# Both batches' tokens side by side, scores from loaded keys and means of V in 32-column tiles

## The chip, the cores and the metric

One Trainium2 chip, one of its cores. The metric is the device time of one execution in microseconds (us), taken as the median of the runs shown.

## The reference

Three blocks in a row, for 2 batches of 768 tokens; all matrices are float32 or float64 cut to what the kernel loads.

- **Attention**, 8 heads of 64. Each token attends to the tokens less than 16 away and to 24 summaries of the sequence, one per block of 32 tokens: the key of a summary is the elementwise maximum of the block's keys, its value the mean of the block's values, and log(32) is added to its score. Scores are scaled by 1/8, one softmax goes over both kinds.
- **Layer 1** (tokens x 512): `h = relu(x @ w_in)`, 1024 wide, cut into u and v; v is normalised over its 512 columns, mixed over tokens by a 768x768 matrix plus a bias per token, and multiplied with u; then `@ w_out`.
- **Layer 2**: `h = relu(x @ w_in2)`, 1024 wide; a convolution of three taps over tokens, per column; `h * sigmoid(conv)`; then `@ w_out2`.

`x @ w_out @ w_in2` has no nonlinearity between, so the kernel multiplies the two weights once (`merge`).

## The kernel before

Dense products are float32 with nearly full precision: each operand is a rounded high part and a low part (the rest), and `mm3` (lines 305 to 311) issues three products for one: high by high, high by low, low by high. `convert` (287 to 303) turns a float64 weight into both parts: one load, a ScalarE or GpSimd multiplication (293, 294), three VectorE steps (296, 298, 300), a cast (284) and a subtraction (278).

Attention goes over 8 pairs of heads (4 per batch), with 2 groups of 6 blocks of 64 queries per pair, so 16 groups.

- `load_kq`, `load_values` (355 to 376): loads of k, q and V's windows, and of v by columns for pairs whose means are not made by TensorE.
- `keys` (378 to 406): `win` copies and scales the windows of 94 keys of a group next to each other (387 on ScalarE, 389 on GpSimd), `top` takes the maxima of 32 keys (397), `put` copies the 24 maxima behind each window (403). So a block has one key matrix of 118 columns.
- `means` (408 to 438): for pairs 0 and 2 (`MEANS_PE`) 12 products with 24 columns of weights (417), all 128 rows of the array; for the others a VectorE sum (424) and a transposition (427). 429, 434 and 436 copy the result.
- `group` (446 to 523): `qk` puts log(32) and the masks into the score bank by small bfloat16 products (460, 466) and adds the score products (473; a float32 product leaves two records in the trace), maxima (477), exponentials with sums (481), reciprocals (487), normalisation (490), transposes (494) and their copies (516), output products (500), high and low parts of the output (521, 522).

Then `f1u`, `f1v` (layer 1's first product), `spatial` (the mixing), `merge`, `i2` (layer 2's first product, its convolution in 684, sigmoid 687, gate 690, high and low part) and `o2` (last product, 709 and 710 write it out). A dense piece is 512 or 256 columns wide: a batch's 768 tokens are cut by `TS` into 512 and 256.

The order on the engines is written out by hand: every `add` call is one job with the engines that could do it; two signs of the string `ORDER` name one job by its number (64 times the first sign's place in `SIGNS` plus the second's), so that counting `add` calls decodes it; a digit of `PICK` names the engine where there is a choice. Each engine, and SP's queue of loads, takes its jobs in that order. Where the plan sees TensorE without work for 0.5 us, it puts in padding: products of constants (720) that nobody reads, the same that warm TensorE up at the start.

Of the kernel before, what the change touches and what calls it, by code (L numbers as in the profile page):

```python
# [29 lines left out]
GB = 6  # L30
GA = GB // 2
NG = NB // GB
MK = 5 * WK + 2 * QB + GA * NS
NZ = NS - 2
# [4 lines left out]
TS = [slice(0, 512), slice(512, S)]  # L39
SLOT = 1536  # L40
MEANS_PE = (0,2)
# [11 lines left out]
    "ACAAABAFAEAgAGADAiAjASATAkAUAhAVAWAXAHAqArALBaAMBbAYBZAIAZA3A4AaBcAbBYAsAcAtAuAvANBiBjAJAlBECTAdA5A6AOBvAwBFCUBwCSA7BkBl"  # L53
    "AKAmBmB8DJAnCRAxAyBxDHCVBGCbA8AzA9A+AoA0BnA-B9DKAPBHCoByBzCcBdDLApBKBLA1A2DIB0BABoCpBpC1BBEgCdEhBCBDCeBqBrB+DRBMCfCgB1B2"
    "BeAQBfBhCqB3B-BIDeBRBgBsEfBSDSDTBJB4ChCrCiCsEeCtCDCEDfDgCWBtBuCXCYCKARB5CjCkC2E0BTBUBVBNCaCuCvBOCFCGCHB6B7BPDUCZClCmCwCx"
    "EnETCMDVDhFODiDWFMDXDYCnCyCAEoEpEUFBC5DMCIBQDwDxDZDrCzC0DNDOCJDyDaDjDkEqErFPFVC6DQE1DPCBDbDlE2DmC3DsC7C8DtDnC9C+AeFNEsDc"
    "DdCCDoFWFXE3E4FiDpEtDqEuC-DuDvDzEiEvD0EjFYEkAfBWCLBXE5D1CNCOF7CPCQD6D7D2D3EwD4E6DADBFjD8ElC4F6ExF8F9EVFCFvGmGDFkGQDCDDEX"
    "DEEZEmEYEaFZEbE7D5D9D+D-EAE8EBDFDGEcE9EEEFEGEHECFFGnFGFzFaFbEIEOEPEQEyGEEzFHGkGdJ5FwEWFIEdFlFcFdERF0FJF1F2F3FeE+E-EDEJEK"
    "ELEMGlESHRFKFLHSFmFQFAFRFDFEGFGRF4FnF5FoENHHHTHIGfFpGGGeFqHJGgGHFSGhGiFrFTFfFgFhGSG6GtGjFUGuGTGUF+FsFtHUHVFuHKHLGIGJHlHb"
    "HcHWGVG7GKGLHdF-HeHmHnGvGwGMGWHoGAGBGNGxGyHXG8HMHNGCFxFyGoHfGXGYIiGZHpHqG9GOGPHrIyIDHvGzHwGaH5HgHsGbGcG0G1H6GpJ9GqIzHxHy"  # L60
    "IjG+G-G2HAGsGrG3HzHOHPG4HtH0H7HBItG5HCH8IEHhHiIFHDHQISJ+H9IIHjHuHYKEJ-HkHZKLIaKAHEINIJITHFHGI0IGIKI1IUILIdIOIeIkIVIPIfIg"
    "IHIMI9I+IbH+KBKCHaH1H2H-IAKDIcI3IBICIXH3KGKFIlI-IWIhKSKHKIIQJlJbIRImJ6KJH4KNKKIYKMI2IZKOI4InKPIoKQJmJvJnJHJIJJJKI5JLIuIv"
    "JAJMKRKjJwJcJoJdJRJSIwJxJTJeIqIrIpJNJOKUKTJBK3K4JUKtJCJPKVKWIsJDJEKXIxLpLrKYJyK5KkKlJpJqI6I7I8LqLsJVJFJWJfJgLtKuK6JGKmLu"
    "JzKnKZKaKvKwKoK7LLLvJXJYJrLwLyJZJhJaLxLzL0JiL1JQJ8L3JjJ0L2KpKxKbKcKdLMLBK8LfLCJsKqL5LgKeLVMrKyLhLWKfMhLiLNL4JkJtL6L7LjLk"
# [12 lines left out]
)
PICK = (
    "001110111100001000001011101001100101011101111100000100000001111101100010001100010000100120001100100110001100110110000010"
    "10000001111011110022000011000000010010010000100100010000110010000100100110100001000000"  # L80
# [121 lines left out]
def block_kernel(ctx, tc, q_in, k_in, vwin, v_in, w_in, w_spT, b_sp, w_outT, w_in2, conv, w_out2, out):  # L202
# [23 lines left out]
    sx, sw, sv0, sar, ssp, stmp = [slots(f"x{b}", NP) for b in range(B)], slots("w", 6), slots("v", 6), slots("a", 14), slots("sp", 1), slots("tmp", 1, 2560)  # L226
    X = [bufs(s) for s in sx]
# [97 lines left out]
    kws, kss, sts = [carve(k, NB * NK) for k in (4, 5)], [carve(k, 32) for k in (4, 5)], [carve(k, 24) for k in (4, 5, 4, 5)]  # L325
    qts, vts = [carve(k, S) for k in (6, 7)], [carve(k, S) for k in (6, 7)]
    kts, ptss, vss = [carve(k, S + 2 * HK) for k in (8, 9)], [carve(10, 128 * GB) for _ in range(2)], [carve(11, 128) for _ in range(2)]
    es = [carve(k, GB * NK + 16) for k in (8, 9, 11, 13)]
    vzs, mask_b, runs_t = [carve(12, NS) for _ in range(2)], carve(12, MK // 2 + 8), carve(12, 2 * NS - 2)
    assert max(used) <= SLOT  # L330
    mask_m = mask_b.ap[:, :MK // 2].bitcast(BF16)
    masks, one, three, logs = mask_m[:, :5 * WK], mask_m[:, 5 * WK:5 * WK + QB], mask_m[:, 5 * WK + QB:5 * WK + 2 * QB], mask_m[:, 5 * WK + 2 * QB:]
# [18 lines left out]

    def vw_tok(j, g, sub):
        return vws[j].tok(g * GB * 128, (g + 1) * GB * 128, sub)

    def load_kq(n):
# [5 lines left out]
        for i, (k0, k1) in enumerate(cuts):  # L361
            dma((k1 - k0) / 2, lambda k0=k0, k1=k1: SP.dma_start(kts[j].ap[:, k0:k1], k_in[b, p][:, k0:k1]), r - 12 + 0.5 * i, writes=[kts[j].tok(k0, k1)])
# [15 lines left out]
    def keys(n):  # L378

        j, r = n % 2, STEP * NG * n  # L380
        for g in range(NG):
            def win(eng, g=g):
                t = kts[j].ap
# [7 lines left out]
            add({"POOL": (0.66, lambda win=win: win(POOL)), "ACT": (0.7, lambda win=win: win(ACT)), "DVE": (0.44, lambda win=win: win(DVE))}, r - 4 + STEP * g,  # L391
                [kts[j].tok(g * GB * QB, (g + 1) * GB * QB + 2 * HK)], [kw_tok(j, g)], lock=True)

        parts = 2 if n < NP and KPART else 1
        for i in range(parts):
            def top(i=i, w=S // parts):
                DVE.tensor_reduce(out=kss[j].ap[:, w // 32 * i:w // 32 * (i + 1)], in_=kts[j].ap[:, HK + w * i:HK + w * (i + 1)].rearrange("p (n k) -> p n k", k=32), op=ALU.max, axis=AX.X)

            w = S // parts
            add({"DVE": (0.14 + w / 960, top)}, r - 4, [kts[j].tok(HK + w * i, HK + w * (i + 1))], [kss[j].tok(w // 32 * i, w // 32 * (i + 1))])  # L400

        def put(eng):
            eng.tensor_scalar(out=kw3(j)[:, :, :NS], in0=kss[j].ap[:, :NS].unsqueeze(1).to_broadcast([128, NB, NS]), scalar1=SCALE, scalar2=0.0,
# [470 lines left out]
```

## Time and profile before

| | us |
|---|---|
| median of 3 runs | 335.71 (335.19 to 336.82) |
| profiled execution | 334.98 |
| its span, first to last instruction | 333.2 |
| TensorE busy in the span | 328.4 |
| VectorE, ScalarE, GpSimd busy | 239.8, 184.6, 82.0 |

The granted clock of TensorE is full over the whole span. Times in the profile are counted from the span's start. Busy TensorE is counted with modelled ends of its products, so that the distance from start to start, not the duration, tells what one costs.

### The profile page before, as it was taken

Reading aid. Unit: us, or ns where it says so; the run is one execution under the profiler, and the core shown is the slowest. Engines: PE = TensorE matmul, PEld = TensorE weight load, DVE = VectorE, ACT = ScalarE, POOL = GpSimd, SP = SyncE. Lnnn points to the kernel's source line nnn. Section 1 sums busy time; section 2 is a strip of 40 time slices with the busy share of each in tenths; the row PEclk is TensorE's granted clock in tenths of the full one; section 3 lists DMA queues with packets and bytes.
Section 4 is the critical chain, followed back from the end, with each engine's and each line's share of the span. In section 5 each row is a group of like instructions: output and inputs, shape, how many; then the busy total and the mean of one; then the engine's idle time right before and its main releaser. Section 6 shows DMA issues by size and latency. Waiting matters only on the chain.

```text
span 333.2 us, 6369 instructions
## 1 busy us (share of the span) xinstructions
PE 328.4 (99%) x2488; PEld 274.6 (82%) x2488; DVE 239.8 (72%) x432; ACT 184.6 (55%) x459; POOL 82.0 (25%) x94
## 2 busy tenths in 40 slices
PE   8999999999999999999999999999999999999996
PEld 3678888888888888888888888888888888888885
DVE  7889899876887599698869687898958542385400
ACT  4999996957245754243325246856664454464221
POOL 4795773334110133200010100351021222011000
PEclk9999999999999999999999999999999999999999
DMA  6999954931253541312302330300000010010023
GB/s 211 317 294 357 249 168 142 275 110 27 63 173 109 211 157 63 128 50 79 126 0 75 116 126 14 114 0 4 0 0 2 0 63 33 0 63 2 0 94 126
DMA packets 13325, 34.49 MB, mean 104 GB/s; under 512 B 1648, under 2 KB 3952, under 8 KB 13296
## 3 DMA queue, kind: packets, MB, share of 16 engines
q1 hardware_dynamic: 13296, 34.10, 32.3%
q8 instruction: 19, 0.31, 0.4%
q14 instruction: 10, 0.08, 0.1%
HBM read 30.95 MB, written 3.15 MB: 102 GB/s over the span
## 4 chain that ended last, share of the span: by engine, by line
PE 97%; DMA 2%; SPq 0%; DVE 0%; issue 0%; ACT 0%
PE late L310 12%; PE late L309 12%; PE late L311 12%; PE mm L309 10%; PE mm L310 9%; PE mm L311 9%; PE xp L500 4%; PE pt L494 4%; PE xp L309 3%; PE xp L310 3%; PE xp L311 3%; PE s L473 3%; PE pt L310 3%; PE pt L309 3%; PE pt L311 3%; PE mm L417 2%
## 5 line engine op out<-in xcount | busy, mean ns | idle before, releaser
L684 DVE SCALAR_TENSOR_TENSOR x<-x,conv_t 128x767 f32<-128x767 f32 x32 | 37.8, 1187 | 14.7 <-ACT x L681 14.3
L481 ACT ACTIVATE a<-s,a 128x118 f32<-128x118 f32 x96 | 33.0, 367 | 1.2 <-DVE a L477 0.9
L298 DVE SCALAR_TENSOR_TENSOR a<-a,a 128x512 uint32<-128x512 uint32 (+1 forms) x32 | 21.6, 674 | 5.5 <-ACT a L293 4.2
L293 ACT ACTIVATE a<-a 128x512 f32<-128x512 f32 (+1 forms) x26 | 17.0, 655 | 10.7 <-DVE w L278 2.8
L278 POOL TENSOR_TENSOR w<-a,w 128x256 fp32r<-128x256 f32 (+1 forms) x11 | 10.4, 949 | 44.2 <-ACT w L284 44.0
L481 ACT ACTIVATION_READ_ACCUMULATOR a<-s,a 128x1 f32 x96 | 20.6, 214 | 0.0
L300 DVE SCALAR_TENSOR_TENSOR a<-a,a 128x512 uint32<-128x512 uint32 (+1 forms) x32 | 19.9, 623 | 0.8
L687 ACT ACTIVATE x<-x 128x768 f32<-128x768 f32 x16 | 13.4, 846 | 12.4 <-DVE x L684 12.3
L490 POOL TENSOR_TENSOR a<-a,a 128x708 f32<-128x708 f32 x13 | 17.9, 1378 | 2.9 <-ACT a L481 1.5
L284 ACT CAST w<-a 128x512 fp32r<-128x512 f32 (+1 forms) x14 | 8.0, 576 | 18.3 <-DVE a L300 18.3
L309 PE MATMUL mm<-w,x 128*128 128x512 f32 x40 | 16.7, 418 | 0.0
L494 PE MATMUL pt<-ident,a 128*118 128x128 f32 x96 | 16.5, 280 | 0.2 <-DVE a L516 0.2
L690 DVE TENSOR_TENSOR x<-x 128x768 f32<-128x768 f32 x11 | 10.5, 956 | 8.4 <-ACT x L687 8.3
L681 ACT ACTIVATE x<-x,conv_t 128x768 f32<-128x768 f32 x16 | 14.7, 939 | 2.6 <-POOL w L278 1.3
L311 PE MATMUL mm<-w,x 128*128 128x512 f32 x40 | 15.7, 392 | 0.0
L310 PE MATMUL mm<-w,x 128*128 128x512 f32 x40 | 15.7, 392 | 0.0
L690 POOL TENSOR_TENSOR x<-x 128x768 f32<-128x768 f32 x5 | 10.1, 2016 | 21.9 <-ACT x L687 21.9
L477 DVE TENSOR_REDUCE a<-s 128x6 f32<-128x708 f32 x16 | 14.1, 883 | 1.8 <-PE s L473 1.5
L500 PEld LDWEIGHTS xp<-a,a 118*64 118x64 f32 x384 | 12.5, 137 | 3.4 <-issue 2.5
L500 PE MATMUL xp<-a,a 118*64 118x64 f32 x384 | 14.7, 226 | 0.0
L309 PE MATMUL mm<-x,w 128*128 128x256 f32 (+1 forms) x40 | 14.7, 367 | 0.0
L494 PEld LDWEIGHTS pt<-ident,a 128*118 128x118 f32 x96 | 10.8, 136 | 4.1 <-issue 0.8
(323 smaller groups left out, 1079.8 us busy)
## 6 DMA issues: line engine op xcount, KB each, us to landing
a<-w_in SPq DMA_DIRECT2D x12, 512.0 KB, 3.8
a<-w_out SPq DMA_DIRECT2D x8, 512.0 KB, 4.0
out<-tmp SPq DMA_DIRECT2D x11, 256.0 KB, 2.0
a<-vwin SPq DMA_DIRECT2D x8, 288.0 KB, 5.9
a<-v_in SPq DMA_DIRECT2D x6, 384.0 KB, 6.7
a<-vwin SPq DMA_DIRECT2D x4, 576.0 KB, 6.7
tmp<-w_spT SPq DMA_DIRECT2D x6, 384.0 KB, 3.4
a<-w_in SPq DMA_DIRECT2D x8, 256.0 KB, 5.1
```

The lines of the kernel that those rows point to most:

```text
L293: mul = {"ACT": (0.2 + n / 1080, lambda: ACT.mul(fu.f(), half(1).bitcast(F32), 2.0 ** -112)), "POOL": (0.12 + n / 1050, lambda: POOL.tenso ...
L298: add({"DVE": (0.16 + n / 960, lambda: DVE.scalar_tensor_tensor(out=last.u(), in0=fu.u(), scalar=0x80000000, in1=last.u(), op0=ALU.bitwise ...
L300: add({"DVE": (0.16 + n / 960, lambda: DVE.scalar_tensor_tensor(out=fu.u(), in0=fu.u(), scalar=3, in1=last.u(), op0=ALU.logical_shift_left ...
L309: PE.matmul(ps, lhsT=lh, rhs=rh, start=first and i == 0, stop=False)
L310: PE.matmul(ps, lhsT=lh, rhs=rl, start=False, stop=False)
L311: PE.matmul(ps, lhsT=ll, rhs=rh, start=False, stop=last and i == n - 1)
L481: ACT.activation(out=e[:, u, :NK], in_=sv[:, u // GA, u % GA], func=AF.Exp, bias=st[:, 0, u:u + 1], scale=1.0, accum_out=sm[:, u, :1])
L490: eng.tensor_tensor(out=e, in0=e, in1=st[:, 1].unsqueeze(2).to_broadcast([128, GB, NK]), op=ALU.mult)
L494: PE.transpose(pt3[:NK, a], e[:, GA * h + a, :NK], ident)
L500: PE.matmul(xp[h * D:(h + 1) * D, k * QB:(k + 1) * QB], lhsT=vw3(j)[:NK, g * GB + k, h * D:(h + 1) * D], rhs=pts[:NK, at:at + QB], start=T ...
L684: DVE.scalar_tensor_tensor(out=ct.f()[:, to], in0=hh.f()[:, of], scalar=conv_t[:, 3 * f + k:3 * f + k + 1], in1=ct.f()[:, to], op0=ALU.mul ...
L690: eng.tensor_tensor(out=ct.f(), in0=hh.f(), in1=ct.f(), op=ALU.mult)
```

## The change

- **Tokens side by side.** The attention output is kept as four buffers of high parts and four of low parts, each with both batches' 768 tokens in a row (1536 columns), in place of a buffer per batch and pair with high and low. The mixing writes its result into the same buffers. Layer 2's first product then runs over all 1536 tokens in three pieces of 512 (`k` = 0, 1, 2); the 256 columns of piece 1 that belong to batch 1 are kept in `hb` and joined later (`join`).
- **Keys without copies.** For the pairs in `DIRECT` (batch 0) `win` and `put` go. A block's scores come from the loaded keys (94 columns) and from the maxima (24 columns) by two products in place of one of 118. Nothing has scaled these keys, so the constants are put in unscaled (`many`, masks of -8e9), the maximum is scaled by one more VectorE step and the exponential scales its input. Four key buffers serve in place of two (two of them lie where the windows of batch 0 were).
- **Means in tiles.** Pair 1 joins pairs 0 and 2 in `MEANS_PE`, so that its v isn't loaded. Pairs 1 and 2 (not 0) use weights of 32 columns in four column tiles of the array, by block number modulo 4; ScalarE copies the 128x128 result and one more product with the matrix `comb` adds the four parts.
- **Buffers and order.** Weights and gate results of the later layers lie elsewhere, `ORDER` and `PICK` are new throughout.

```diff
+DIRECT = (0,1,2,3)
+MEANS_F = (0,)
-TS = [slice(0, 512), slice(512, S)]
+TS = [[slice(0, 512), slice(512, S)], [slice(0, 256), slice(256, S)]]
-MEANS_PE = (0,2)
+MEANS_PE = (0,1,2)
...
-    kws, kss, sts = [carve(k, NB * NK) for k in (4, 5)], [carve(k, 32) for k in (4, 5)], [carve(k, 24) for k in (4, 5, 4, 5)]
+    kws, kss, sts = [carve(k, NB * NK) for k in (4, 5)], [carve(k, 32) for k in (4, 5, 4, 5)], [carve(k, 24) for k in (4, 5, 4, 5)]
...
+    def kt(n):
+        return kts[n % (4 if n in DIRECT else 2)]
...
-        for g in range(NG):
+        for g in range(0 if n in DIRECT else NG):
             def win(eng, g=g):
...
+        if n not in DIRECT:
+            add({"POOL": (0.44, lambda: put(POOL)), "DVE": (0.33, lambda: put(DVE))} if n else {"DVE": (0.33, lambda: put(DVE))}, r - 3, [ks.tok()], [kws[j].tok(sub="s")], lock=True)
...
+        elif n in MEANS_PE:
+            part, ps, quad = mms[1][:, :128], xp[:NS, 384:512], vts[j].at(0, 128)
+            for g in range(NG):
+                def mm(g=g):
+                    for blk in range(g * GB, (g + 1) * GB):
+                        q = blk % 4 * 32
+                        PE.matmul(part[q:q + 32], lhsT=runs_t.ap[:NK, NZ - 2 * blk:NZ - 2 * blk + 32], rhs=vw3(j)[:NK, blk],
+                                  start=blk < 4, stop=blk >= NB - 4, skip_group_check=True)
...
+            add({"ACT": (0.28, lambda: ACT.copy(quad.ap, part)), "DVE": (0.26, lambda: DVE.tensor_copy(quad.ap, part))}, r + 1.7, [tok("mm1")], [quad.tok()])
+            add({"PE": (0.3, lambda: PE.matmul(ps, lhsT=comb.ap, rhs=quad.ap, start=True, stop=True))}, r + 1.8, [quad.tok(), comb.tok()], [m], mode="F")
...
-                for c in range(2):
-                    blk = g * GB + 2 * a + c
-                    for h in range(2):
-                        rows = slice(h * D, (h + 1) * D)
-                        PE.matmul(s[c * QB:(c + 1) * QB, h, a * NK:(a + 1) * NK], lhsT=qts[j].ap[rows, blk * QB:(blk + 1) * QB],
-                                  rhs=kw3(j)[rows, blk], start=False, stop=True, skip_group_check=True)
+                for part in (0, 1) if direct else (2,):
+                    for c in range(2):
+                        blk = g * GB + 2 * a + c
+                        for h in range(2):
+                            rows = slice(h * D, (h + 1) * D)
+                            k0, k1 = ((NS, NK), (0, NS), (0, NK))[part]
+                            rhs = (kt_.ap[rows, blk * QB:blk * QB + WK], ks.ap[rows, :NS], kws[j].ap[rows, blk * NK:(blk + 1) * NK])[part]
+                            PE.matmul(s[c * QB:(c + 1) * QB, h, a * NK + k0:a * NK + k1], lhsT=qts[j].ap[rows, blk * QB:(blk + 1) * QB],
+                                      rhs=rhs, start=False, stop=True, skip_group_check=True)
 
         def row_max():
-            DVE.tensor_reduce(out=st[:, 0], in_=sv, op=ALU.max, axis=AX.X, negate=True)
+            DVE.tensor_reduce(out=low if direct else st[:, 0], in_=sv, op=ALU.max, axis=AX.X, negate=True)
+            if direct:
+                DVE.tensor_scalar(out=st[:, 0], in0=low, scalar1=SCALE, scalar2=None, op0=ALU.mult)
...
-    def i2(b, f):
+    def i2(k, f, to):
+        fs, xs = slice(f % 4 * 128, (f % 4 + 1) * 128), slice(512 * k, 512 * (k + 1))
...
+    def layer2(b, f):
+        hh, ct = hidden()
+        if b == 0:
+            i2(0, f, [(0, hh.at(0, 512))])
+            r = i2(1, f, [(0, hh.at(512, 256)), (256, hb[f])])
+        else:
...
+            r = i2(2, f, [(0, hh.at(256, 512))])
+            add({"ACT": (0.41, lambda: join(ACT)), "POOL": (0.37, lambda: join(POOL)), "DVE": (0.25, lambda: join(DVE))}, r - 1, [hb[f].tok()], [hh.tok(0, 256)], lock=True)
+        conv_gate(b, f, hh, ct, r)
...
+        DVE.memset(many, 0.0)
...
+            DVE.memset(many[h * QB:h * QB + 3], 1.0 / SCALE)
```

Decoded, SP's queue begins before with k (two loads), w_in, q, k (two), q; after with k (two), q, k, q, k, w_in. TensorE's order of batch 0's first groups (`qk` scores, `tr` transposes, `pv` output products, by group from 0) is before: qk0, qk1, qk2, means of pair 0, qk3, tr0, the rest of these means, tr0, qk4, tr1, pv0, tr1, qk5, tr2, pv1, tr2, qk6, tr3, transposition of pair 1's sums, tr3, qk7, pv2, tr4, means of pair 2, pv3. After, it is the same up to pv1, then means of pair 1, qk6, tr2, the adding product, tr3, qk7, tr3, pv2, one dense piece, means of pair 2, pv3, tr4.

## Rows read from the trace of the kernel before

**Rows 1.** The page: busy time, share of the span and instructions per engine.

```profile
PE 328.4 (99%) x2488; PEld 274.6 (82%) x2488; DVE 239.8 (72%) x432; ACT 184.6 (55%) x459; POOL 82.0 (25%) x94
```

**Rows 2.** The page: the chain that ended last, by engine.

```profile
PE 97%; DMA 2%; SPq 0%; DVE 0%; issue 0%; ACT 0%
```

**Rows 3.** Waits of TensorE, whole span: us in total, times, longest.

```profile
PE s L473 <- DMA a<-q_in: 0.5, 1, 0.5
```

**Rows 4.** Busy us by stretch: PE, PEld, DVE, ACT, POOL, clock, DMA share, GB/s.

```profile
9.15:31.28 22.13, 21.95 (x407) 16.71 (x407) 19.93 (x49) 21.59 (x108) 16.49 (x22) 1.00 1.00 313
36.58:100.00 63.42, 63.42 (x713) 53.27 (x713) 53.38 (x114) 43.17 (x152) 24.86 (x33) 1.00 0.50 145
```

**Rows 5.** The chain in order of time, 7 to 37 us: start, us, what.

```profile
8.16 1.19 PE mm L720 x5
...
9.62 0.60 PE s L473 x24
...
18.35 0.85 PE xp L500 x24
...
21.88 0.54 PE mm L720 x2
...
24.10 0.12 PE xp L427
...
27.64 2.73 PE mm L417 x24
```

**Rows 6.** TensorE's timeline, 24 to 25 us.

```profile
24.05 0.59 PE L720 MATMUL mm<-ones 128*128 128x512 bf16 x2
```

**Rows 7.** The timeline of all engines, first 8 us (SPq issues loads).

```profile
1.64 0.42 SPq L292 DMA_DIRECT2D a<-w_in  x1
...
5.93 0.31 DVE L403 TENSOR_SCALAR a<-a 128x288 f32<-128x288 f32 x1
...
6.28 0.28 PE L460 MATMUL s<-a 64*64 64x72 bf16 x4
...
7.33 0.84 PE L473 MATMUL s<-a,a 64*64 64x118 f32 x24 [0.54 <-DMA a<-q_in]
```

**Rows 8.** TensorE's timeline, one undisturbed group.

```profile
13.67 0.23 PE L460 MATMUL s<-a 64*64 64x72 bf16 x4
13.72 0.29 PE L466 MATMUL s<-a 64*64 64x282 bf16 x4
13.85 0.77 PE L473 MATMUL s<-a,a 64*64 64x118 f32 x24
14.55 0.54 PE L494 MATMUL pt<-ident,a 128*118 128x128 f32 x3
```

**Rows 9.** Groups by line and shape, 0 to 100 us: busy, mean ns | idle before.

```profile
L387 ACT ACTIVATE a<-a 128x564 f32<-128x564 f32 x9 | 6.1, 678 | 1.3 <-DMA a<-k_in 1.3
L424 DVE TENSOR_REDUCE a<-a 128x24 f32<-128x768 f32 x6 | 5.6, 932 | 0.0
L487 DVE RECIPROCAL a<-a 128x6 f32<-128x6 f32 x16 | 2.9, 183 | 0.2
```

**Rows 10.** TensorE's timeline: first and last of 30 and of 16 dense products.

```profile
107.49 0.40 PE L309 MATMUL late<-w,x 128*128 128x512 f32 x1
...
114.09 0.39 PE L311 MATMUL mm<-w,x 128*128 128x512 f32 x1
...
328.12 0.28 PE L311 MATMUL mm<-a,sp 128*128 128x256 f32 x1
...
329.92 0.28 PE L311 MATMUL mm<-a,sp 128*128 128x256 f32 x1
```

**Rows 11.** Busy us by stretch again, early layer 2.

```profile
220.00:240.00 20.00, 20.00 (x116) 17.59 (x115) 18.53 (x20) 12.56 (x20) 3.94 (x2) 1.00 0.01 2
240.00:260.00 20.00, 20.00 (x101) 16.93 (x100) 13.78 (x14) 10.33 (x17) 3.79 (x2) 1.00 0.00 1
```

**Rows 12.** Groups by line and shape, whole span, the gate on VectorE.

```profile
L690 DVE TENSOR_TENSOR x<-x 128x768 f32<-128x768 f32 x11 | 10.5, 956 | 8.4 <-ACT x L687 8.3
```

More of the change, by code (lines that the diff above doesn't have):

```diff
@@ L659, in block_kernel, with hidden @@
+    hb = units(bufs(sar[5:6], 2), 256, 6) + [TMP.at(2048 + 256 * f, 256) for f in range(2)]
+    tmps[512] = tmps[512][:4]
+    T = bufs(sv0[:3], 1)
     nT = [0]
-    def i2(b, f):
+    def hidden():
         t_ = T[nT[0] % 3]
         nT[0] += 1
-        hh, ct = t_.at(0, S), t_.at(S, S)
-        y = yb[b][f]
-        hi, lo = y.at(0, S), y.at(S, S)
-        fs = slice(f % 4 * 128, (f % 4 + 1) * 128)
-        for h in range(2):
-            hs = TS[h]
-            n = hs.stop - hs.start
-            ps, m = bank()
-            for c in range(4):
-                def mm(c=c, ps=ps, hs=hs, n=n):
-                    g = G[b][c].r()
-                    w = wp(c, f // 4)
-                    mm3(ps()[:, :n], [((w[0].r()[:, fs], w[1].r()[:, fs]), (g[:, hs], g[:, S + hs.start:S + hs.stop]))], first=c == 0, last=c == 3)
-                w = wp(c, f // 4)
-                r = dense(n, cost(n), mm, [w[0].tok(), w[1].tok(), G[b][c].tok(hs.start, hs.stop), G[b][c].tok(S + hs.start, S + hs.stop)], [m])
-            add({"ACT": (0.18 + n / 1200, lambda ps=ps, hs=hs, n=n: ACT.activation(out=hh.f()[:, hs], in_=ps()[:, :n], func=AF.Relu))}, r, [m], [hh.tok(hs.start, hs.stop)])
+        return t_.at(0, S), t_.at(S, S)
@@ new lines, in i2, with mm @@
+    def i2(k, f, to):
+        fs, xs = slice(f % 4 * 128, (f % 4 + 1) * 128), slice(512 * k, 512 * (k + 1))
+        ps, m = bank()
+        w = wp(0, f // 4)
+        for c in range(4):
+            def mm(c=c, w=wp(c, f // 4)):
+                mm3(ps(), [((w[0].r()[:, fs], w[1].r()[:, fs]), (XH[c].r()[:, xs], XL[c].r()[:, xs]))], first=c == 0, last=c == 3)
+            w = wp(c, f // 4)
+            r = dense(512, cost(512), mm, [w[0].tok(), w[1].tok(), XH[c].tok(xs.start, xs.stop), XL[c].tok(xs.start, xs.stop)], [m])
+        for at_, h in to:
+            add({"ACT": (0.18 + h.n / 1200, lambda at_=at_, h=h: ACT.activation(out=h.f(), in_=ps()[:, at_:at_ + h.n], func=AF.Relu))}, r, [m], [h.tok()])
+        return r
@@ L729, in pool_constants @@
             for base, step in ((0, 1), (2 * HK, -1)):
-                POOL.affine_select(out=tiles[rows, 1], in_=tiles[rows, 1], compare_op=ALU.is_ge, fill=-1.0e9, base=base, pattern=[[step, WK]], channel_multiplier=-step)
+                POOL.affine_select(out=tiles[rows, 1], in_=tiles[rows, 1], compare_op=ALU.is_ge, fill=-8.0e9, base=base, pattern=[[step, WK]], channel_multiplier=-step)
     def level_constants():
@@ L773, in block_kernel @@
     add({"POOL": (2.15, pool_constants)}, -100, writes=[mask_b.tok(sub="m"), tok("ident")])
-    add({"DVE": (2.0, level_constants)}, -100, writes=[runs_t.tok(), mask_b.tok(sub="l")] + [sts[j].tok() for j in range(4)])
+    add({"DVE": (2.3, level_constants)}, -100, writes=[runs_t.tok(), mask_b.tok(sub="l")] + [sts[j].tok() for j in range(4)])
     add({"DVE": (1.1, mask_tiles)}, -99, [tok("ident")], [mask_b.tok(sub="m")])
+    add({"DVE": (0.2, lambda: DVE.tensor_reduce(out=comb.ap, in_=ident.rearrange("p (j r) -> p r j", r=32)[:, :NS], op=ALU.add, axis=AX.X))}, -97, [tok("ident")], [comb.tok()])
     for j in sorted({n % 2 for n in MEANS_PE}):
```

171 lines of the change are left out of this document (91 added, 80 removed).

## The prediction

> **What bounds the kernel now.** I read the busy shares first: TensorE is busy for 328.4 of 333.2 us [rows 1]. A busy TensorE need not be a full one, so the chain that ended last comes next: 97% of it is TensorE [rows 2], and the longest wait of TensorE once it has begun is 0.5 us, for the first load of q [rows 3]. So the end is set by how long TensorE's queue is, and a part of the change is worth what it takes out of that queue, plus what TensorE starts earlier.
>
> The table of stretches says where other engines could take over [rows 4]. From 36.58 to 100 us TensorE has no gap at all and ScalarE is busy 43 of 63 us. But from 9.15 to 31.28 us, while batch 0's attention runs, ScalarE is busy 21.59 of 22.13 us, VectorE 19.93 and the DMA engines all of the time. TensorE's 21.95 us there are partly padding: the chain in order of time shows five L720 products at 8.16 us, 1.19 us of constants between the first two groups' scores (five more follow the second group), and two more at 21.88 and at 24.05 us [rows 5, 6]. Up to about 25 us the pace is thus set by exponentials and copies, after it by TensorE. Eight groups (two per pair of heads) make up a batch.
>
> **The first products.** Today the first load of w_in is issued at 1.64 us, ahead of q; masks and key maxima are ready at 6.28, when the first small products start, but the score products start only at 7.33 [rows 7]. In an undisturbed group they start 0.18 us after the first small one (13.67 and 13.85 [rows 8]). The new order string, decoded by counting the jobs, issues k, k, q and leaves w_in until after the second pair's keys. I take 7.33 - 6.28 - 0.18 = 0.87 us off. On VectorE the copy of pair 0's maxima (0.31 us) goes and three small fills for the new constant come, which I put at the same: nothing. At best the whole 1.05 goes, at worst 0.4 because VectorE's chain (fills, masks, maxima) ends later.
>
> **Scores from loaded keys.** For batch 0 every score product of 118 columns becomes one of 94 and one of 24. Today's 24 records of a group take 0.60 us [rows 5]. By columns the two sorts take 0.48 and 0.12, together no more than now: the lower bound, 0. If each of the 24 new records costs what a record costs now, 0.60/24 = 25 ns, they add 0.60 - 0.12 = 0.48 per group. The nearest row is the four products of 72 columns that start at 13.67, with the next sort at 13.72: 0.05 us for four [rows 8], or 0.30 for 24. I take this: 0.48 + 0.30 - 0.60 = +0.18 per group, +1.44 for eight; ends 0 and +3.8. What this buys is not on TensorE: of the window copies four leave ScalarE, 678 ns each [rows 9], and four leave GpSimd. Against that each group's maximum gets a second VectorE step on 128x6 to scale it; a reciprocal of that size takes 183 ns [rows 9], 1.5 us in all. It stands between scores and exponentials, and behind it on VectorE wait the sums, copies and low parts of the groups before.
>
> **Means of V.** Pair 2's means take 2.73 us now, 24 records with 24 of 128 columns of the array in use [rows 5]. In four tiles of 32 columns a quarter, 0.68, is the least; the output products, which share the array two by two, need 0.85 for 24 records [rows 5]. I take 0.85, plus 0.10 on either side for the change of tiling (score products begin at 13.85, run 0.60, and the next begins at 14.55 [rows 5, 8]), plus two records at 2.73/24 us for the product that adds the four parts: 1.28. Pair 2 saves 1.45. Pair 1 has today one transposition of 0.12 and will have the same 1.28: +1.16. In the new order these products stand where the two later paddings stood, between the second output products and group 6; that time is twice 0.54, or 1.08 [rows 5, 6]. So pair 1 costs +0.08 net while that cover lasts, 1.16 if it is gone. The adding product waits for a ScalarE copy that stands behind group 5's exponentials, and it writes the bank of the output products, so also for group 1's low part on VectorE; behind it on TensorE stand group 3's transposes and group 7's scores. Pair 1's sum on VectorE (932 ns [rows 9]) and its load of 384 KB go; at the 313 GB/s of that stretch [rows 4] everything later on SP's queue lands 1.2 us sooner. No product waits for a load after the first, so I cost this at nothing. The means need V's windows sooner: 21 loads, 4.9 MB, stand on SP's queue up to the second half of pair 1's, about 16 us at that rate from the first arrivals on, and the products come at about 22.
>
> **Pieces of 512.** Layer 2's first product now runs per batch in 512 and 256 columns and will run over both batches in three of 512. From 107.49 to 114.09 us 29 steps of 512 take 6.60 us, 0.2276 each; from 328.12 to 329.92, 15 steps of 256 take 1.80, 0.120 each [rows 10]. Per slice f and c, six of either sort take 2.086 us, nine of 512 take 2.048; times 32, **-1.2 us**. This is certain, since nothing else has to be true for it than that TensorE stays full. The quarter of batch 1 that is computed early is parked and copied back: eight small copies, four on ScalarE and four on VectorE, beside TensorE.
>
> **The rest at nothing.** Splitting X into high and low buffers changes addresses. Spatial pieces are reordered, not resized. The new pick string puts all 32 gates and low parts of layer 2 on VectorE, where GpSimd now has nine; at 0.956 us each [rows 12] that is 8.6 us more. The cover is thinnest from 220 to 240 us, where VectorE is busy for 18.53 of 20 us; the next 20 leave it 6.2 free [rows 11], and batch 0's share of the nine is five, 4.8 us.
>
> **The sum.** -0.87 + 1.44 - 1.45 + 0.08 - 1.2 = -2.0 us. The profiled execution took 334.98 us (span 333.2 and 1.8 around it), which becomes 333.0; the median of the three runs shown is 335.71, 0.73 above, and that is what I correct: **333.7 us**, own range 332.6 to 334.7.
>
> **Rivals.** *The early stretch belongs to VectorE and ScalarE.* Between the first and the last maximum of batch 0 the new order gives VectorE eight scalings, +1.5; a whole pair's maximum (of the sum's shape) moves in where pair 1's sum goes, and copies change places. Less the 0.87 of the start, batch 0's exponentials come 0.6 later than now, TensorE's savings there turn into waits for copies, and start, scores and means together give +0.6 instead of -0.8: -0.6, 335.1. For it speaks ScalarE's 98% in [rows 4]; against it, that ScalarE is relieved of 2.7 us. *The loads set the early stretch.* The DMA share is 1.00 there, and fewer, earlier loads let the padding between the first scores go as well: twice 1.19, 331.3. Against it: one wait of 0.5 us for a load, and the padding fills the time of an exponential. *Small products have a fixed pitch.* If no record starts within 25 ns of the one before, a group's 48 records take 1.20 us, +0.60 each and +4.8 instead of +1.44: 337.1, slower than before. It decides from (1.44 + 2.0)/8 = +0.43 per group on. The four products in 0.05 us [rows 8] speak against it. *VectorE late in layer 2*: if the five operations of batch 0 fall where only 1.5 us are free [rows 11], low parts come 3.3 us late and output products wait for them: 337.0. Against it, the free 6.2 us right behind.
>
> The Trainium skill, "TensorE: Matmul & The Clock Gate", section "Wait — 56ns, not 53.3ns?", states the third rival as a rule: start-to-start never drops below about 25 ns however small the product. By that rule the sum would be +1.4 instead of -2.0; the row with four starts in 0.05 us does not follow it, at least for products on four separate tiles.
>
> **Chances.** The forecast 0.46, the engines' stretch 0.32, the loads 0.12, the pitch 0.06, VectorE late 0.04. A measurement of this kernel can tell about 0.5% from no change: under 334.0 counts as faster, above 337.4 as slower. Faster takes three quarters of the forecast, the loads and a little of the first rival: 0.50. Same takes the rest of the forecast, most of the first rival and half of the pitch: 0.43. Slower 0.07. The range 331.1 to 336.5 takes in the loads' case, the first rival and most of the unknown of the score products.
>
> **What would show it.** Right: score products of batch 0 starting near 6.5 us; a group's scores 0.78 us instead of 0.60; pair 2's means near 0.9; no L720 products after the first dozen or so but those between the first three groups; TensorE without waits beyond 30 us; layer 2's products all 512 wide at 0.228. Wrong: TensorE waiting for VectorE's or ScalarE's copies between 15 and 35 us (first rival), groups at 1.2 us (third), or gaps ahead of the output products of layer 2 (fourth).

## The result and the profile after

The changed kernel takes **337.51 us** (median; 336.43 to 338.59), the kernel before 335.14: ratio 1.0069, 95% interval 1.0050 to 1.0089. That is 2.4 us slower where 2.0 us faster was forecast, and above the range. The profiled execution took 336.79 us, its span is 335.0 (before 333.2).

The page of the changed kernel: busy time, the granted clock in 40 slices, the chain by engine.

```profile
PE 327.1 (98%) x2603; PEld 271.7 (81%) x2603; DVE 239.5 (72%) x457; ACT 185.2 (55%) x460; POOL 60.3 (18%) x78
...
PEclk9899999999999999999999999999999999999999
...
PE 93%; DVE 2%; ACT 2%; issue 1%; POOL 0%; DVEq 0%; ACTq 0%
```

TensorE is busy 1.3 us less than in [rows 1], in a span 1.8 us longer: it now stands idle. Its share of the chain fell from 97% [rows 2] to 93%, "issue" (an engine without any wait that the profile shows) has 1%, and the second slice has less than the full clock. TensorE's waits in the changed kernel, where [rows 3] had one of 0.5 us after the warm-up:

```profile
PE s L489 <- DVE a L801: 1.4, 1, 1.4
PE mm L768 <- DVE mhalf L762: 1.0, 1, 1.0
PE xp L528 <- issue: 0.6, 2, 0.4
PE s L499 <- DVE a L403: 0.5, 1, 0.5
PE xp L528 <- POOL a L457: 0.5, 1, 0.5
PE xp L440 <- DVE xl L551: 0.4, 1, 0.4
PE pt L522 <- ACT a L545: 0.2, 1, 0.2
```

Stretches of the changed kernel, columns as in [rows 4]; the last four answer to [rows 4, 11]:

```profile
6.90:10.30 3.40, 3.21 (x97) 3.16 (x98) 2.13 (x5) 0.50 (x3) 0.42 (x1) 0.54 0.95 287
9.15:31.28 22.13, 21.24 (x535) 16.60 (x530) 18.85 (x49) 19.52 (x101) 15.10 (x17) 0.97 0.81 249
36.58:100.00 63.42, 62.92 (x753) 52.15 (x752) 51.60 (x113) 44.48 (x152) 28.32 (x35) 1.00 0.53 158
220.00:240.00 20.00, 20.00 (x90) 16.57 (x89) 19.03 (x25) 15.77 (x26) 0.00 (x0) 1.00 0.14 49
240.00:260.00 20.00, 20.00 (x90) 16.56 (x89) 19.78 (x24) 17.29 (x30) 0.00 (x0) 1.00 0.00 1
```

From 9.15 to 31.28 us TensorE has 535 matrix records where it had 407; ScalarE is busy 19.5 us where it was 21.6, and the eighth group's exponentials end at 32.73 us in place of 31.28. Late in layer 2 TensorE waits for nothing. So the loss lies ahead of 50 us. The chain in order of time there, and the first score products on TensorE's timeline:

```profile
2.99 1.22 DVE a L798
4.23 1.33 DVE a L798
...
7.09 1.44 PE s L499 x40
...
8.84 1.51 PE s L499 x48
10.35 2.19 PE mm L768 x9
...
12.82 0.80 PE s L499 x48
...
20.70 0.41 issue
...
30.05 0.21 issue
...
31.38 0.79 PE mm L433 x24
...
34.59 0.48 DVE xl L551
```

```profile
6.22 0.36 PE L499 MATMUL s<-a,a 64*64 64x94 f32 x8
7.09 1.44 PE L499 MATMUL s<-a,a 64*64 64x24 f32 x40 [0.52 <-DVE a L403]
```

Three things are to be seen. At the start VectorE's two mask casts (L798) take 2.58 us; the warm-up has only 9 products and ends before 4.5, TensorE waits 1.4 and 0.5 us, and the granted clock from 6.90 to 10.30 us is 0.54, that is mostly the lower level of 1.2 GHz: the last 40 records of the first group's scores take 1.44 us and all 48 of the second 1.51, where the third takes 0.80. All eight runs of this kernel have a mean granted clock of 0.993 to 0.995. Around 20 and 30 us TensorE stops in the middle of its output products without any wait that the profile shows (issue; 0.41 and 0.21 us). And at 34 us the adding product waits for VectorE's low part.

**What the issue gaps are.** Counting TensorE's instructions in the trace, the gaps that no wait explains lie at no. 706 and 1218 here, and in the experiments at 450, 706, 962 and 1218: always a multiple of 256 apart. The DMA queue of kind "instruction" brings packets of 16 KB, and each such gap ends 1.3 to 1.7 us after one has landed. So TensorE, as I read it, had run out of instructions. The Trainium skill, "Runtime: NRT & Kernel Launch", section "Instruction fetch mechanics", says that instructions are refilled in blocks of 16 KiB, 256 of them, by the sequencer's own DMA, which agrees, and that crossing into a new block is mostly hidden. That holds for the kernel before, where no gap lies at a block's end; here two boundaries show.

### The profile page after: what moved, and what is told of

Its sections match the earlier page's. It is cut to its first block, busy times and chain, and to the rows that moved or that the text cites. A ratio compares the mean times of both kernels' runs of the same rounds, so it can differ in the third digit from the quotient of the medians.

```text
span 335.0 us, 6609 instructions
## 1 busy us (share of the span) xinstructions
PE 327.1 (98%) x2603; PEld 271.7 (81%) x2603; DVE 239.5 (72%) x457; ACT 185.2 (55%) x460; POOL 60.3 (18%) x78
## 4 chain that ended last, share of the span: by engine, by line
PE 93%; DVE 2%; ACT 2%; issue 1%; POOL 0%; DVEq 0%; ACTq 0%
PE late L310 12%; PE late L311 12%; PE late L312 12%; PE mm L310 9%; PE mm L311 9%; PE mm L312 9%; PE xp L528 4%; PE pt L522 3%; PE s L499 3%; PE xp L311 3%; PE xp L310 3%; PE xp L312 3%; PE pt L311 3%; PE pt L310 3%; PE pt L312 3%; ACT a L509 1%
## 5 line engine op out<-in xcount | busy, mean ns | idle before, releaser
L716 DVE SCALAR_TENSOR_TENSOR v<-v,conv_t 128x767 f32<-128x767 f32 x32 | 32.5, 1014 | 6.0 <-ACT v L713 5.5
L311 PE MATMUL late<-xl,a 128*128 128x512 f32 x48 | 18.7, 389 | 0.0
L310 PE MATMUL late<-xh,a 128*128 128x512 f32 x48 | 18.7, 389 | 0.0
L312 PE MATMUL late<-xh,a 128*128 128x512 f32 x48 | 18.7, 389 | 0.0
L719 ACT ACTIVATE v<-v 128x768 f32<-128x768 f32 x16 | 13.5, 844 | 9.1 <-DVE v L716 9.0
L722 DVE TENSOR_TENSOR v<-v 128x768 f32<-128x768 f32 x16 | 15.2, 954 | 3.6 <-ACT v L719 3.4
L499 PE MATMUL s<-a,a 64*64 64x24 f32 (+2 forms) x576 | 15.5, 250 | 0.5 <-DVE a L403 0.5
L757 ACT COPY tmp<-late 128x512 f32<-128x512 f32 x7 | 4.1, 589 | 21.0 <-PE late L312 21.0
L713 ACT ACTIVATE v<-v,conv_t 128x768 f32<-128x768 f32 x16 | 15.0, 937 | 0.9 <-DVE w L279 0.5
L499 PEld LDWEIGHTS s<-a,a 64*64 64x64 f32 x576 | 14.6, 146 | 0.7 <-DVE a L403 0.7
L310 PE MATMUL mm<-xh,w 128*128 128x256 f32 (+1 forms) x40 | 14.5, 362 | 0.0
```

The source lines that it names most:

```text
L310: PE.matmul(ps, lhsT=lh, rhs=rh, start=first and i == 0, stop=False)
L311: PE.matmul(ps, lhsT=lh, rhs=rl, start=False, stop=False)
L312: PE.matmul(ps, lhsT=ll, rhs=rh, start=False, stop=last and i == n - 1)
L499: PE.matmul(s[c * QB:(c + 1) * QB, h, a * NK + k0:a * NK + k1], lhsT=qts[j].ap[rows, blk * QB:(blk + 1) * QB], rhs=rhs, start=False, stop= ...
L716: DVE.scalar_tensor_tensor(out=ct.f()[:, to], in0=hh.f()[:, of], scalar=conv_t[:, 3 * f + k:3 * f + k + 1], in1=ct.f()[:, to], op0=ALU.mul ...
```

## The experiments

Times are medians; the kernel before stood at 334.8 to 335.2 in all comparisons. The theories are named in the texts on record: S (the start), L (a loop too long because of the scaling step), later I (instruction blocks).

**The start.** Three kernels: a warm-up of 18 products; GpSimd's two fills later; both.

```diff
-    add({"PE": (WARM * 0.43 + 0.5, lambda: warm(WARM))}, ...)
+    add({"PE": (WARM * 0.43 + 0.5, lambda: warm(18))}, ...)
```

> Edit: 18 warm-up products in place of 9, nothing else. In the changed kernel TensorE is idle from 4.49 to 6.07 us and has half its clock from about 6.9 to 10.3 us; the scores of groups 0 and 1 take 1.44 and 1.51 us. Theory S (the start: TensorE stands idle, its clock halves, and the delay of group 2 runs on through batch 0): the clock is full throughout, the two groups' scores take 0.8 us each, group 2's exponentials start 0.6 to 1.3 us sooner than at 14.89 us, and the end comes 1.0 to 1.9 us sooner (335.6 to 336.5 against 337.5 of the changed kernel). Theory L (the loop of scores, maximum, scaling, exponentials is too long for two score banks, whatever the start): the end gains at most 0.7 us, and TensorE still waits between 20 and 48 us.

> Edit: GpSimd's two fills of V's rows (1.37 us each) come behind its first weight multiplication in place of ahead of everything, and no padding after the first ten microseconds of the plan (as in the changed kernel). Theory S: VectorE's copies of the masks take about 1.6 us or less in place of 2.58, the key maxima and the first scores come 0.9 to 1.2 us sooner (scores at about 6.0), TensorE's idle time after the warm-up shrinks to 0.7 us or so and its clock may stay full; the end comes 1.0 to 1.9 us sooner. Theory L: the start gains 1 us but the end at most 0.7.

> Edit: the longer warm-up and the later fills together. Theory S: full clock, and the end 1.5 to 2.2 us sooner than the changed kernel (335.3 to 336.0), level with the kernel before within 0.5. Theory L: at most 0.8 us sooner, with the same waits from 20 to 48 us.

Measured 337.76 (ratio 1.0093, 1.0064 to 1.0121), 336.53 (1.0054, 1.0034 to 1.0074) and 336.56 (1.0050, 1.0030 to 1.0069). The start itself mended as foreseen: full clock in all three profiles, and without the fills the casts, on VectorE's timeline, take

```profile
2.99 0.41 DVE L798 CAST a<-ident 64x64 bf16<-64x64 f32 x2
```

But the gain is 1 us at best, and the intervals overlap with that of the changed kernel; the longer warm-up alone gains nothing. The chain of the longer warm-up shows where the rest went: what TensorE won at the start it lost at its instruction no. 706.

```profile
19.66 1.52 issue
```

**The scaling step left out.**

```diff
-                DVE.tensor_scalar(out=st[:, 0], in0=low, scalar1=SCALE, scalar2=None, op0=ALU.mult)
```

> Edit: VectorE's step that scales the maximum of each direct group (8 in all) is left out; the exponentials take the unscaled maximum, so this kernel leaves out a part of the computation. The start stays as it is. Theory L: each of the eight loops from scores to exponentials is 0.27 us shorter, ScalarE's waits for VectorE (7.6 us in all in the changed kernel) shrink by 1.5 us or more, TensorE's waits between 20 and 48 us shrink, and the end comes 1.0 to 1.5 us sooner. Theory S: less than 0.5 us.

Measured 338.42 (ratio 1.0098, 1.0073 to 1.0123): no gain, so nothing here speaks for L. It isn't refuted either, because this profile (340.18 us, the longest of the six runs) lost time elsewhere: the nine padding products behind the second group took 3.61 us in place of 2.25, and at no. 706 TensorE stood idle for 1.44 us (1.66 from start to start), with half the clock behind it.

```profile
10.33 3.61 PE L766 MATMUL mm<-ones 128*128 128x512 bf16 x9
```

```profile
23.65:27.00 3.35, 3.35 (x67) 2.84 (x68) 0.56 (x1) 2.44 (x11) 0.68 (x2) 0.50 0.36 107
```

**More instructions on the kernel before.** Score products in two, and in three:

```diff
-                for c in range(2):
+                for k0, k1 in ((NS, NK), (0, NS)) if n < NP else ((0, NK),):
...
+                for k0, k1 in ((NS, 71), (71, NK), (0, NS)) if n < NP else ((0, NK),):
```

> Edit, on the kernel before: batch 0's score products are cut in two (94 and 24 columns) as in the changed kernel, but from the copied keys; no other part of the change. Theory I (new, from the last four runs): TensorE's instructions are loaded by DMA in packets of 16 KB, one per 256 instructions; in the four kernels TensorE's gaps that no wait explains lie at its instructions no. 450, 706, 962 and 1218, always 256 apart, and end 1.3 to 1.6 us after such a packet has landed; where batch 0's groups issue 48 more instructions each, TensorE reaches a block's end before the next has come, while the DMA engines are full of loads. By I this kernel shows such gaps too and takes 1.6 us (0.20 per group, eight groups) and 0.5 to 2 us more than the kernel before: 337.0 to 338.7 against 335. Theory L (VectorE and ScalarE are late because of the change's own extra steps): the extra 1.6 us alone or less, 336.0 to 336.7, without gaps at block ends.

> Edit, on the kernel before: batch 0's score products are cut in three (24, 47 and 47 columns, from the copied keys) in place of two as in the earlier run; 96 more TensorE instructions per group than the kernel before. The run with two gave +2.05 us, of which 1.6 are work. If only work counts: 1.6 more for the second cut, 338.4 to 338.9. Theory I: a block of 256 instructions then lasts TensorE about 4 us, and while the loads run one comes every 5.5 to 6 us; with some 7 blocks in batch 0's attention the gaps at block ends sum to 4 us or more, and the time is 341 or more.

Measured 337.19 (1.0075, 1.0044 to 1.0105) and 343.10 (1.0244, 1.0214 to 1.0274). The first cut costs 2.05 us, 1.6 of them work; the second 5.9 more with 1.6 of work. With three products the view of waits, the chain and two stretches show:

```profile
PE s L474 <- issue: 3.5, 2, 2.2
```

```profile
12.32 1.29 issue
...
17.09 2.17 issue
```

```profile
16.90:19.25 2.35, 0.19 (x12) 0.09 (x5) 0.00 (x0) 0.63 (x4) 0.43 (x1) 0.98 0.71 242
19.30:22.50 3.20, 3.20 (x17) 2.37 (x17) 1.67 (x5) 1.97 (x10) 1.37 (x1) 0.50 0.72 222
```

Two gaps at no. 450 and 706, and behind the second, for 3.2 us, the clock at its lower level. Nothing else was changed, so the added products alone, with their work and their instructions, do this. There were two long gaps and not one per block, fewer than expected. Half the clock is not needed for most of it: one of the four runs had a mean granted clock of 1.0 and took 342.43.

**Fewer instructions on the changed kernel.** Summary scores of two blocks by one product:

```diff
+                    PE.matmul(s[:, h, a * NK:a * NK + NS], lhsT=qts[j].ap[rows, q0:q0 + 2 * QB], rhs=ks.ap[rows, :NS],
```

> Edit, on the changed kernel: the 24 summaries' scores of two neighbouring blocks come from one product with 128 columns of weights in place of two with 64, so batch 0's groups issue 24 instructions fewer each (192 in all, three quarters of a block of 256). Theory I: the gaps at block ends shrink by half or go, and the end comes 1.0 to 2.0 us sooner (335.5 to 336.5 against 337.5). Theory L: VectorE's and ScalarE's steps are the same, so the gain is at most what TensorE's work shrinks by, 0 to 0.8 us.

342.90 (1.0211, 1.0177 to 1.0245), inconclusive: no gaps at block ends, but in its profile TensorE is at half clock through the padding up to 16 us, and group 2 starts at 16.46 us, where the changed kernel has it at 12.47. Two runs with a mean granted clock of 0.999 took 343.3 and 343.6, so this run stays unexplained. Then the summary products left out, on the mended start and on the kernel as it is:

```diff
-                for part in (0, 1) if direct else (2,):
+                for part in (0,) if direct else (2,):
```

> Edit, on the kernel with the longer warm-up and the later fills: the second product (24 summary columns) of batch 0's groups is left out, so this kernel leaves out a part of the computation and issues 48 TensorE instructions fewer per group, 384 in all; its TensorE work shrinks by 1.6 us. Theory I: the gaps at block ends (1.23, 0.65 and 0.39 us in the profile of the kernel it is made from) go as well, and the time is 332.6 to 333.6 against 336.6. Without I (the gaps have another cause): 334.6 to 335.2, with gaps.

> Edit: the same products left out of the changed kernel as it is, with its start at half clock. The difference to the kernel with the mended start is what the start costs once the instructions come in time. Theory S+I (two causes that hide each other): 1.0 to 1.9 us more than the run with the mended start, 333.8 to 335.2. If the start costs nothing by itself: the same within 0.4.

335.97 (1.0031, 1.0006 to 1.0056) and 335.42 (0.9998, 0.9976 to 1.0020). The changed kernel gains 2.1 us; with the mended start it gains only 0.6. Both texts missed: a gap of 0.6 to 0.7 us from start to start stays at no. 706, and TensorE waits for exponentials, low parts and means instead. The 2.1 are in part the clock: five of the twelve runs without the products have a mean granted clock of 0.994 to 0.995, like every run of the changed kernel, and their median of 336.08 is 1.4 us below it, no more than the 1.6 of work; the other seven have 0.999 or 1.0 and a median of 334.50. The profile of the second kernel has the full clock at its start too, so this pair does not tell what a start at half clock costs.

**A load moved.** Keys of batch 1 behind later loads.

> Edit, on the changed kernel: the first keys of batch 1 (399 KB), which stand in SP's queue ahead of pair 3's keys of batch 0, are loaded after the weights of the third quarter, and the steps that use them (VectorE's maximum of 0.93 us, GpSimd's copies) come later too. Same instructions on TensorE. Theory I: between 10 and 20 us the DMA engines have 1.3 us less to do, the instruction packets start up to 1.3 us sooner after the block before has begun (3.2 us in the changed kernel), the gap at instruction 706 shrinks by as much, end 0.5 to 1.2 us sooner. Theory L: VectorE has 0.93 us less to do ahead of group 4's maximum, which gives 0.3 to 0.9 us too, but with the gap at 706 as before.

339.64 (1.0132, 1.0103 to 1.0162): wrong in sign. The DMA engines stayed full all the same (share 1.08 from 8.32 to 14.08 us); the packet due at no. 450 started at 14.08 us in place of 12.41, TensorE had no product there for 2.4 us and went on 1.5 us after the landing. This agrees with I, but I had not foreseen it, and why the packet came later still is open.

**The pieces alone, and then the keys alone.** Batch 0 in the order of the kernel before, layer 2 as changed; then scores from loaded keys on top of it:

```diff
-DIRECT = (0,1,2,3)
-MEANS_F = (0,)
-MEANS_PE = (0,1,2)
+DIRECT = ()
+MEANS_F = (0, 2)
+MEANS_PE = (0, 2)
```

> Edit: the changed kernel's buffers and its layer 2 in pieces of 512, but batch 0's attention as in the kernel before (window copies, means of pairs 0 and 2 the old way, pair 1's by VectorE, the old order up to pair 3's output products). This measures the pieces alone. By the working of the prediction: 1.2 us less than the kernel before, 333.8 against 335.0. If TensorE's queue isn't what sets layer 2's end: no difference, 335. Theories I and L say the same here: no gaps at block ends, as in the kernel before.

> Edit, on the kernel with the pieces alone: batch 0's scores from the loaded keys, in two products, with the scaling step and without the window copies, in the order of the kernel before; means the old way. This is the keys' part of the change alone. Work of TensorE +1.6 us. Theory I with nothing else: 333.1 + 1.6 + 0.4 to 1.0 for gaps at block ends = 335.1 to 335.8. If the keys' part carries the whole loss (4.4 us between the pieces alone and the changed kernel): 337 or more. If the relief of ScalarE gives something back: under 334.7.

The pieces alone: **333.12** (0.9928, 0.9900 to 0.9956), 2.0 us faster than before, the best kernel of the study. Its page and stretches:

```profile
PE 326.2 (98%) x2391; PEld 269.5 (81%) x2391; DVE 238.3 (72%) x452; ACT 187.3 (56%) x461; POOL 62.8 (19%) x84
...
PE 97%; DMA 1%; SPq 0%; DVE 0%; issue 0%; ACT 0%; ACTq 0%
```

```profile
9.15:31.28 22.13, 21.91 (x407) 16.76 (x407) 20.14 (x50) 21.70 (x108) 16.55 (x22) 1.00 0.98 302
```

The early stretch is as in [rows 4]; TensorE is busy 2.2 us less over the span than in [rows 1]. With the keys' part on top: 337.56 (1.0078, 1.0049 to 1.0106). **On top of the pieces this part costs 4.4 us**, as much as lies between the pieces alone and the changed kernel. Its chain, stretches and DMA queues from 13.6 to 15 us:

```profile
13.82 0.24 PE s L499 x12
14.05 2.15 issue
16.21 1.46 PE s L499 x24
...
28.86 0.54 DVE a L545
...
37.70 0.56 DVE xl L551
38.40 0.92 PE xp L528 x24
```

```profile
8.80:13.70 4.90, 4.66 (x133) 3.58 (x125) 4.42 (x13) 4.50 (x26) 1.79 (x2) 1.00 1.07 273
...
21.00:22.80 1.80, 1.80 (x70) 1.59 (x72) 1.68 (x5) 0.30 (x2) 1.80 (x2) 1.00 0.05 18
...
13.80:16.20 2.40, 0.25 (x16) 0.15 (x4) 0.80 (x3) 1.73 (x11) 0.00 (x0) 1.00 1.03 364
16.25:19.60 3.35, 3.35 (x45) 2.71 (x46) 1.82 (x6) 1.08 (x6) 0.55 (x1) 0.50 1.04 353
```

```profile
q1 hardware_dynamic: 276, 0.45, 99.4%
q8 instruction: 1, 0.02, 5.4%
```

TensorE passed into the block before (no. 194) at 8.77 us, but the next packet started only at 13.69, landed at 14.90, and the products went on at 16.21. In between the DMA engines were full (share 1.07). At no. 706, after a stretch with share 0.05, the packet came at once (22.82, with the block's end at 22.86). That the loads delay the packets is read from such rows; taking loads away was not tried. Behind the gap of 2.15 us the clock is at 0.50 for 3.35 us, so that what follows, transposes and pair 0's means, runs at half speed too.

Start against start with the pieces alone, this profile is 0.1 us ahead at the fourth group's constants (13.47 and 13.55 us), 3.2 behind at the first transposes (17.59, 14.43), 4.9 behind at the fourth output products (35.06, 30.20), 5.5 at the fifth (38.40, 32.88), and no further: the spans are 337.1 and 331.6. The step from 4.9 to 5.5 is a wait of 0.60 us for VectorE, over which the chain runs from 28.86 to 38.40. The profiled execution took 338.90 us, 1.3 more than the median. It and one other run (339.18) have a mean granted clock of 0.995; the other four have 1.0 and took 336.41 to 337.93, with a median of 337.1. So about 4.0 us are lost without the half clock too, and it adds about 1.9 where it comes.

**The means.** Pair 2 in tiles on the kernel with the pieces alone; then V's load earlier; then ScalarE's copy earlier:

```diff
-MEANS_F = (0, 2)
+MEANS_F = (0,)
-            part, ps, quad = mms[1][:, :128], xp[:NS, 384:512], vts[j].at(0, 128)
+            part, ps, quad = mms[1][:, :128], mms[1][:NS, 128:256], vts[j].at(0, 128)
```

> Edit, on the kernel with the pieces alone (batch 0 as before): pair 2's means in four tiles of 32 columns, with the adding product in the bank of the tiles. By the prediction's working TensorE's queue is 1.45 us shorter: 331.7 against the 333.1 of the pieces alone, if TensorE sets the pace there. By its first rival (the stretch up to 31 us belongs to ScalarE and VectorE, TensorE's savings turn into waits): 332.8 to 333.4, and TensorE waits 1 us or more between 27 and 36 us.

> Edit, on the kernel with the pieces and pair 2's means in tiles: the second half of pair 1's windows of V stands 7 places further ahead in SP's queue. In the profile of the kernel it is made from, pair 1's output products wait 1.9 us for this load, because pair 2's means no longer fill that time. If that load is what ate the saving: 331.5 to 332.5 (the 333.1 of the pieces alone less up to 1.45). If ScalarE and VectorE set that stretch: 333 to 333.6, and the wait is for them.

> Edit, on the kernel with the pieces, pair 2's means in tiles and the earlier V load: ScalarE copies the tiles ahead of group 7's exponentials in place of behind them, and one step of the first dense product stands behind the adding product. In the profile of the kernel it is made from, TensorE waits 1.9 us for that copy and its clock falls to half behind it. If the tiles' saving (1.45 us) can be had at all: 331.7 to 332.6 (333.1 with the old means). If ScalarE's exponentials set the stretch up to 31 us: 333.0 to 333.6, TensorE waits elsewhere before 33 us.

334.44 (0.9982, 0.9962 to 1.0003), 335.22 (1.0008, 0.9991 to 1.0025), 334.73 (0.9995, 0.9968 to 1.0021): all slower than 333.12, also when only the runs at the full mean clock are taken. The longest waits of TensorE are, in the first, for V's windows, in the second for ScalarE's copy, and in the third (timeline) for the bank of the output products, which VectorE empties only at 34.06 us with a group's low part; the profile names the step behind that (L512):

```profile
PE xp L528 <- DMA a<-vwin: 1.9, 1, 1.9
```

```profile
PE mm L440 <- ACT a L439: 1.7, 1, 1.7
```

```profile
34.21 0.92 PE L528 MATMUL xp<-a,a 118*64 118x64 f32 x24 [1.56 <-DVE a L512]
```

Each wait removed let the next one through. On the changed kernel, with the mended start, two more runs: the adding product in its own bank, and the old means again.

> Edit, on the kernel with the longer warm-up and the later fills: the product that adds the four parts of the means writes the bank of the tiles in place of the bank of the output products, so it no longer waits for VectorE's low part of a group (0.65 us at 35 us in every profile of the changed kernel). If that wait is on the path: 0.4 to 0.7 us less than 336.6. If the time is lost to something that is late anyway (exponentials, instructions): no change within 0.4.

> Edit, on the kernel with the longer warm-up and the later fills: means of pairs 1 and 2 the old way again (VectorE's sum and one transposition for pair 1, 12 products over the whole array for pair 2), everything else as in the changed kernel. TensorE's work grows by 0.7 us. If the new means bring what they take off TensorE: 337.3. If they bring nothing because their waits (the adding product for VectorE, 0.65 us) eat it: 336.3 to 336.9. If they cost: under 336.2.

336.60 (1.0049, 1.0027 to 1.0070): no change; in place of the 0.65 us for VectorE's low part a dense piece now starts 0.63 us late, because ScalarE still has to copy from its bank. 338.91 (1.0111, 1.0085 to 1.0137): the old means cost 2.35 us in this order, against 0.7 of work, and none of the three cases had that; the profile has a gap of 1.25 us at no. 706. So what tiles are worth hangs on the order around them.

**The first products alone.** w_in's first load behind q, on the kernel with the pieces.

> Edit, on the kernel with the pieces alone: the first load of w_in stands behind q and pair 1's keys on SP's queue, and the steps that take this weight apart behind the first two groups' maxima; paddings as before. This is the prediction's step on the first products by itself, 0.87 us: scores of group 0 near 6.5 in place of 7.15 us, all exponentials 0.6 to 0.9 us sooner, 332.3 to 332.6 against 333.1. If the paddings or the loads that follow set the pace: 333.1 within 0.3, and the first exponentials no sooner or the gain gone by 20 us.

333.45 (0.9957, 0.9940 to 0.9973): no gain. Score products start at 6.35 us in place of 7.18, the first exponential at 9.02 as before, because ScalarE now waits for the later weight first:

```profile
8.11 0.44 ACT L294 ACTIVATE a<-a 128x256 f32<-128x256 f32 x1 [3.66 <-DMA a<-w_in]
8.46 0.66 ACT L393 ACTIVATE a<-a 128x564 f32<-128x564 f32 x1
9.02 0.34 ACT L509 ACTIVATE a<-s,a 128x118 f32<-128x118 f32 x1
```

## Why the prediction was wrong

**The sum in its own terms:** the keys' part +4.4 (forecast +1.44), the pieces -2.0 (forecast -1.2); from 337.56 with both to the changed kernel's 337.51, means, new order and start together, 0.0 (forecast -0.87, -1.45 and +0.08). That is +2.4. These are the steps of one path, and not shares that the changed kernel itself shows: its gaps at block ends are 0.6 us together, its half clock lies at the start, and without the second products it gains 2.1, or 1.4 at the same clock. No run divides its loss among start, waits, gaps and work.

- **The step that failed first is the price of the scores from loaded keys.** The prediction counted what a record costs TensorE, and got that right: 48 records in 0.80 us where 24 took 0.60, +0.20 per group where +0.18 was taken. It held that the columns and the pitch were the whole price. Each group also issues 48 more instructions, and these arrive by DMA, in blocks of 256, while loads fill the engines [rows 4]. On top of the pieces the part cost 4.4 us in place of 1.44: in its profile 1.6 us of work, a gap of 2.15 at a block's end, half the clock behind it and 0.6 of waiting for VectorE; at full clock still 4.0. On the kernel before, the split alone cost 2.05, with one gap of 0.9. No rival had this. How near the limit was could have been counted beforehand: in the kernel before the packets of the first five blocks landed 1.9 to 5.1 us ahead of the first instruction in them, and where TensorE had to wait for one it went on 1.3 to 1.7 us after the landing.
- **First products:** wrong. Eight of the first 48 records ran at 6.22, but the other forty waited for VectorE's key maxima until 7.09 and ended at 8.53, where the kernel before was done at 8.17: the worse end of that step (VectorE's chain ends later) came true and more. The changed start has a second GpSimd fill beside VectorE's casts, and a warm-up that ends early. By itself the earlier score brought nothing in the last run, in an order in which ScalarE waited for the later weight.
- **Pair 2:** the size on TensorE was right (0.79 us of tiles and 0.40 of adding, 1.28 taken), the gain was not: on the kernel with the pieces the shorter products turned into waits, as the first rival said, one each for a load, for ScalarE and for VectorE. That rival had the place of the waits, and gave 335.1.
- **Pieces of 512:** right, and undersized by 0.8. One padding product fewer (0.22) is part of it; the profiles' spans differ by 1.6 only, so the rest stays within what the runs can tell.
- **The rest at nothing:** right for layer 2. VectorE is busy 19.03 and 19.78 of 20 us there and TensorE waits for nothing; the fourth rival fell.
- **The third rival** (25 ns per record, 1.20 us a group) fell: 0.80 us for 48 is 17 ns each. The floor of about 25 ns from start to start that the Trainium skill states, "TensorE: Matmul & The Clock Gate", section "Wait — 56ns, not 53.3ns?", does not hold here, for small products on four separate tiles.

Open: how the remaining zero divides between the new order, the means and the start, what delays the packets (that it is the loads is read from the rows alone), and what VectorE's scaling step costs.

## What to carry to other kernels

Count instructions as well as cycles: a change that splits products in two doubles their instructions, and in this kernel, in a stretch where loads fill the DMA engines, the instructions came late without any semaphore to show it. "Issue" gaps in the chain, a fixed number of instructions apart, are its mark. And where other engines set the pace, take work off TensorE only if the chain through those engines becomes shorter too: the tiles did not make it so, the pieces of 512 stood where TensorE alone was the bound.

## What had not been expected of the hardware

- An idle TensorE can pay twice. In the profiles with the keys alone, with three score products, with the earlier V load and without the scaling step, idle times of 2.15, 2.17, 1.68 and 1.44 us were followed by 3.2 to 3.4 us at a granted clock of 0.50; 1.52 us with the longer warm-up and 1.56 us with ScalarE's earlier copy were not, so the length of the gap alone does not decide. Runs of one kernel with and without a lowered mean clock show the price: with two score products eight runs at 1.0 took 336.5 to 337.7 us and three at 0.994 to 0.995 took 339.8 to 340.4. Stretches of the earlier V load:

```profile
28.90:30.80 1.90, 0.22 (x9) 0.08 (x5) 1.69 (x5) 1.84 (x12) 0.00 (x0) 1.00 1.04 417
31.80:35.20 3.40, 3.40 (x59) 2.77 (x47) 2.60 (x9) 1.95 (x4) 2.51 (x3) 0.50 1.06 265
```

- Two casts of 64x64 on VectorE take 0.41 us alone and 2.58 us while GpSimd fills memory. The Trainium skill, "GPSIMD Engine Reference", section "Key points", says that VectorE's instructions in a 2-port mode, or with two inputs in SBUF, contend with GpSimd for the interfaces that the two share; no run here shows in which mode the casts ran, and the factor of six is this case's.
